# A gated recurrence and its feed-forward: stores in one transfer each, and one more block transposed by DMA

## The chip, the cores and the metric

The kernel runs on one core of a Trainium2 chip. The metric is the device time of one execution, in microseconds (us). Three runs of the kernel before took 178.43, 179.19 and 180.09 us; their median is 179.19.

## What is computed

A gated linear recurrence over 768 steps runs for 4 batches of 8 heads with 48 features each; its output, with the heads side by side as 384 columns, goes through a feed-forward layer with a SiLU:

```python
def _attn_ref(q, k, v, f_logit):                       # each (4, 8, 768, 48)
    f = 1.0 / (1.0 + np.exp(-f_logit))
    for t in range(S):
        state = f[:, :, t, :, None] * state + np.einsum('bhd,bhe->bhde', k[:, :, t], v[:, :, t])
        y[:, :, t] = np.einsum('bhd,bhde->bhe', q[:, :, t], state)

def _moe_ref(x, w_in, w_out):                          # x (3072, 384), w_in (384, 2048), w_out (2048, 384)
    h = x @ w_in
    g = h * (1.0 / (1.0 + np.exp(-h)))
    return g @ w_out
```

All inputs and the output are float32; the kernel's matmuls take bf16.

## The kernel before

The 768 steps are cut into 3 windows of 256, so that with 4 batches there are 12 blocks (block D is window D // 4 of batch D % 4). In a block each of 128 partitions holds two neighbouring steps (r = 0, 1), and the partitions fall into two chunks of 64 (f = 0, 1), each of 128 steps. Within a chunk the recurrence is done as masked matrix products; between chunks a state is carried on.

The order of all work is written out by hand, as a list of tokens (PLAN). A token is a kind, a block and, for most, the head half or chunk or column group; after an @ stands the engine (s SyncE's queue, v VectorE, a ScalarE, p GpSimd, called POOL). `emit` turns each into instructions, in the order of the list; each engine runs its own instructions in that order, and waits where data or buffers aren't ready. `uses` names the buffers that a token touches. Buffers come from pools of fixed size (SLOTS), freed at the last use; PSUM has eight banks.

The steps of a block, with the lines in the kernel before:

- ldf, ldk, ldq, ldv load a block's gate logits, k, q and v (L276). Block 0 and 1 are loaded in halves of four heads.
- E, L, F1 (L278 to L282), SA (L284), CS (L286 and L289, TensorE), IA, A, AX (L292 to L296), AM (L298) make the decay factors. E to AX are ScalarE's.
- K1 (L300) and Q1 (L302) scale k and q; KI (L306) and QG (L311) write them as bf16 to a tile named qk.
- TQ (L320) turns that tile on TensorE, eight transpositions of 128 x 128 into PSUM, and QC copies them to SBUF (L272). TD (L324) does the same as one DMA transpose on SyncE's queue. Blocks 0 to 3 go by TQ and QC, blocks 4 to 11 by TD.
- SC (L333) forms the scores of a head half, AT (L339) masks them, Y (L347) multiplies by v (cast by VB), YS (L354) adds the carried state's part, YC (L272) copies a chunk's output to the tile yb.
- YT (L362) turns yb on TensorE in three transpositions a chunk and XC copies them (L272); YD (L366) does it as one DMA transpose. Blocks 0 to 3 go by YT and XC, blocks 4 to 11 by YD.
- DP (L372), SD (L377) and SU (L379) carry the state to the next chunk.
- MI (L388) multiplies by a 256-column group of w_in: 8 tokens of 6 matmuls for a block. SI (L392) is the SiLU of that group, from PSUM to the bf16 tile hT. MO (L396) multiplies by w_out: 4 matmuls a token, four tokens for each of two output tiles of 128 rows. OC (L272) copies such a tile from PSUM, and SO (L402) stores both tiles of a block, or one.
- WI and WO load the weights in eight pieces each, and CI and CO cast them to bf16.
- W is a row of matmuls on an empty tile (L416) that fills waits of TensorE early in the run; its result is not used.

Rows of hT come out with the even steps of a chunk ahead of the odd ones, since that is how the transposed y lies. So an output tile holds them in that order, and SO needs two transfers, one for each r, of 64 partitions each (L401 and L402):

```python
dst = out.rearrange("(b w f p r) n -> b w r p f n", b=B, f=2, p=64, r=2)
for r in range(2):
    E.dma_start(out=dst[b, w, r][:, fs], in_=T[0][64 * r:64 * r + 64, fs])
```

All stores and loads are issued by SyncE. Whenever the order passes from an exponential or logarithm to a SiLU or back, ScalarE loads another function table (L420).

Of the kernel before, what the change touches and what calls it, by code (L numbers as in the profile page):

```python
# [36 lines left out]
    QG.2.1@v QG.2.0@v CI.7@v K1.2.1@v CI.4@p K1.2.0@v KI.2.1@v KI.2.0@v AM.2@v CI.0@v SA.3.0@v SA.3.1@p SU.1.1@p
    CO.0@p VB.2@p CO.5@p MI.0.1 MI.0.3 MI.0.5 MI.1.3 MI.0.2 MI.1.5 SI.0.1 SI.1.1 SI.1.3 SI.0.2 SI.1.5 MI.0.4 SI.0.4
    MI.0.7 MI.1.7 MI.1.4 SI.1.7 SI.0.5 TQ.2.1 TQ.2.0 CI.6@v QC.2.0@v QC.2.1@v CO.1@v MI.1.0 MI.0.0 SI.0.3 SI.1.4
    SI.1.2 SI.1.0 MI.0.6 SI.0.6 SI.0.0 MI.1.6 SC.2.1 SC.2.0 AT.2.1 AT.2.0 SI.1.6 CO.3@a CO.2@a SI.0.7 MO.1.0.0  # L40
    MO.0.1.0 MO.0.0.0 MO.1.1.0 MO.1.0.1 MO.0.0.1 MO.0.1.1 DP.2 Y.2.0 Y.2.1 SU.2.0@v CO.4@v MO.1.1.1 YS.2.1 CS.3.0
    SD.2.1 YC.2.0@v YC.2.1@v MO.1.0.2 MO.0.0.2 MO.0.1.2 YT.2.1 YT.2.0 XC.2.1@v XC.2.0@v IA.3.0 E.4.0 L.4.0 MO.1.1.2
    CS.3.1 SA.4.0@v MI.2.4 CS.4.0 CO.6@p CO.7@v MO.1.0.3 OC.1.0@v MO.0.1.3 MO.1.1.3 E.4.1 L.4.1 AX.3.1 F1.3.1 F1.3.0
    A.3.0 IA.4.0 A.4.0 SU.2.1@p SA.4.1@p CS.4.1 IA.3.1 A.3.1 IA.4.1 AX.4.0 AX.3.0 AX.4.1 F1.4.0 MO.0.0.3 K1.3.0@p
    K1.3.1@p KI.3.1@p Q1.3.0@v OC.0.1@v OC.1.1@v Q1.3.1@v QG.3.0@v AM.3@v QG.3.1@v AM.4@v ldq.4@s ldk.4@s MI.2.7
    MI.2.6 MI.2.3 A.4.1 F1.4.1 OC.0.0@a MI.2.1 MI.2.0 SI.2.7 SI.2.6 SI.2.0 SI.2.1 KI.3.0@v TQ.3.0 MI.2.5 TQ.3.1
    Q1.4.0@v Q1.4.1@v QG.4.1@v K1.4.1@p KI.4.1@p QG.4.0@v QC.3.1@v ldv.3@s ldf.6@s ldv.4@s ldf.5@s MI.2.2 MO.2.0.0
    SI.2.3 SI.2.4 SI.2.5 SI.2.2 QC.3.0@v K1.4.0@p KI.4.0@p VB.3@p VB.4@p SC.3.1 AT.3.1 SC.3.0 AT.3.0 MO.2.1.0
# [433 lines left out]
```

## Time and profile before

| What | us |
|---|---|
| median of three runs (lowest, highest) | 179.19 (178.43, 180.09) |
| the profiled execution, its own time | 178.64 |
| its span, from the first to the last instruction | 176.9 |
| TensorE matmuls busy | 168.7 (95% of the span) |
| ScalarE busy | 120.9 (68%) |
| VectorE busy | 103.0 (58%) |
| POOL busy | 62.1 (35%) |

The granted TensorE clock was 0.995 over the span. In the profile PE is TensorE's matmuls, PEld its weight loads (they overlap matmuls), DVE is VectorE, ACT ScalarE, POOL GpSimd and SP SyncE, whose queue issues the transfers (SPq). A group's row gives line, engine, operation, the tiles written and read, shapes and count, then busy us and mean ns of one, then the idle time of the engine ahead of them and what ended it. A row of the timeline gives start, length, engine, line and how many; consecutive instructions of a kind are merged. A row of stretches gives start and end, then each engine's busy time and count, the granted clock, the busy share of the 16 DMA engines, and GB/s.

### The profile page before, as it was taken

Reading aid. Unit: us, or ns where it says so; the run is one execution under the profiler, and the core shown is the slowest. Engines: PE = TensorE matmul, PEld = TensorE weight load, DVE = VectorE, ACT = ScalarE, POOL = GpSimd, SP = SyncE. Lnnn points to the kernel's source line nnn. Section 1 sums busy time; section 2 is a strip of 40 time slices with the busy share of each in tenths; the row PEclk is TensorE's granted clock in tenths of the full one; section 3 lists DMA queues with packets and bytes.
Section 4 is the critical chain, followed back from the end, with each engine's and each line's share of the span. In section 5 each row is a group of like instructions: output and inputs, shape, how many; then the busy total and the mean of one; then the engine's idle time right before and its main releaser. Section 6 shows DMA issues by size and latency. Waiting matters only on the chain.

```text
span 176.9 us, 5606 instructions
## 1 busy us (share of the span) xinstructions
PE 168.7 (95%) x2280; PEld 127.9 (72%) x2280; DVE 103.0 (58%) x252; ACT 120.9 (68%) x281; POOL 62.1 (35%) x106
## 2 busy tenths in 40 slices
PE   7598999999999999999999999999999999999990
PEld 5486789766796688857688767688676788875550
DVE  6269987636798996297484498880369710000320
ACT  5868999854799899888699985599902128772001
POOL 6387561133593683013728017507501000000000
PEclk9999999999999999999999999999999999999998
DMA  5999999999908959997999996999999461000094
GB/s 127 294 310 344 358 342 363 351 340 242 320 13 154 319 143 212 200 293 191 190 189 220 236 313 169 197 253 229 250 161 171 108 136 44 4 0 0 5 241 113
DMA packets 82234, 36.02 MB, mean 204 GB/s; under 512 B 74016, under 2 KB 82208, under 8 KB 82208
## 3 DMA queue, kind: packets, MB, share of 16 engines
q1 hardware_dynamic: 82208, 35.66, 81.4%
q8 instruction: 18, 0.29, 0.7%
q14 instruction: 8, 0.07, 0.1%
HBM read 25.17 MB, written 4.72 MB: 169 GB/s over the span
## 4 chain that ended last, share of the span: by engine, by line
PE 83%; issue 8%; DVE 3%; DMA 2%; ACT 2%; SPq 1%
PE ps L388 36%; PE ps L396 29%; PE ps L333 3%; PE ps L347 3%; PE ps L354 3%; PE ps L372 3%; DMA wide<-in_f_logit_dram 2%; PE ps L416 2%; PE ps L320 1%; PE ps L286 1%; DVE atm L339 1%; PE ps L362 1%; ACT e L278 1%; ACT lf L280 1%; SPq L276 1%
## 5 line engine op out<-in xcount | busy, mean ns | idle before, releaser
L396 PE MATMUL ps<-w_out_sb,hT 128*128 128x384 bf16 x384 | 67.5, 326 | 0.0
L388 PE MATMUL ps<-xT,w_in_sb 128*128 128x256 bf16 x576 | 65.5, 273 | 0.0
L388 PEld LDWEIGHTS <-w_in_sb 128*128 128x128 bf16 x576 | 55.6, 98 | 7.2
L392 ACT ACTIVATE hT<-ps 128x512 bf16<-128x512 f32 x96 | 49.9, 618 | 9.2 <-PE ps L388 8.7
L396 PEld LDWEIGHTS <-hT 128*128 128x128 bf16 x384 | 35.7, 98 | 22.0
L339 DVE TENSOR_TENSOR atm<-ps,mask 128x512 bf16<-128x512 f32 x48 | 30.0, 682 | 8.9 <-PE ps L333 7.6
L272 DVE COPY o<-ps 128x384 f32<-128x384 f32 x18 | 9.9, 554 | 29.1 <-issue 21.2
L306 POOL TENSOR_TENSOR qk<-wide,ia 128x192 bf16<-128x192 f32 x36 | 21.5, 621 | 11.0 <-ACT hT L392 7.2
L379 POOL TENSOR_TENSOR st<-sd,al 128x384 bf16<-128x384 f32 x12 | 10.2, 850 | 19.7 <-DVE sd L377 16.6
L311 DVE TENSOR_TENSOR qk<-wide,ps 128x192 bf16<-128x192 f32 x48 | 14.2, 347 | 3.7 <-ACT ps L294 3.2
L272 ACT CAST yb<-ps 128x384 bf16<-128x384 f32 x12 | 5.4, 480 | 14.5 <-PE ps L354 11.8
L278 ACT ACTIVATE e<-wide 128x384 f32<-128x384 f32 x24 | 12.3, 523 | 2.2 <-DMA wide<-in_f_logit_dram 2.0
L302 DVE SCALAR_TENSOR_TENSOR wide<-e,wide 128x192 f32<-128x192 f32 x24 | 11.2, 483 | 3.6 <-ACT f L282 3.6
L284 POOL TENSOR_TENSOR s<-lf 128x192 bf16<-128x192 bf16 x15 | 8.8, 593 | 11.8 <-ACT lf L280 10.4
L280 ACT ACTIVATE lf<-e 128x384 bf16<-128x384 f32 x24 | 12.0, 520 | 0.5
L377 DVE TENSOR_TENSOR sd<-ps,st 128x384 f32<-128x384 f32 x16 | 8.6, 552 | 6.1 <-PE ps L372 6.0
L272 ACT COPY o<-ps 128x384 f32<-128x384 f32 x6 | 2.9, 490 | 13.3 <-issue 12.4
L416 PE MATMUL ps<-idle 128*128 128x256 bf16 x72 | 10.8, 305 | 1.3 <-DVE idle L428 1.3
L420 ACT ACT_TABLE_LOAD x9 | 11.5, 1283 | 0.2
L300 POOL TENSOR_TENSOR wide<-wide,f 128x192 f32<-128x192 f32 x13 | 8.2, 631 | 8.4 <-ACT f L282 4.0
L292 ACT ACTIVATE ia<-ps 128x192 f32<-128x192 f32 x24 | 7.6, 333 | 4.2 <-PE ps L289 4.2
L416 PEld LDWEIGHTS <-idle 128*128 128x128 bf16 x72 | 7.3, 109 | 3.0 <-DVE idle L428 1.2
(59 smaller groups left out, 157.4 us busy)
## 6 DMA issues: line engine op xcount, KB each, us to landing
out_dram<-o SPq DMA_DIRECT2D x22, 192.0 KB, 3.1
wide<-in_f_logit_dram SPq DMA_DIRECT2D x10, 384.0 KB, 4.8
wide<-in_q_dram SPq DMA_DIRECT2D x10, 384.0 KB, 4.6
wide<-in_k_dram SPq DMA_DIRECT2D x10, 384.0 KB, 5.7
wide<-in_v_dram SPq DMA_DIRECT2D x10, 384.0 KB, 4.6
wide<-in_moe_w_in_dram SPq DMA_DIRECT2D x8, 384.0 KB, 6.3
wide<-in_moe_w_out_dram SPq DMA_DIRECT2D x8, 384.0 KB, 7.0
wide<-in_f_logit_dram SPq DMA_DIRECT2D x4, 192.0 KB, 3.3
```

The costliest lines, as they stand in the source:

```text
L272: copy = lambda o, i: E.copy(o, i) if eng == "a" else E.tensor_copy(o, i)
L278: nc.scalar.activation(T[1][:, hs], T[0][:, hs], AF.Exp, scale=-1.0)
L280: nc.scalar.activation(T[1][:, hs], T[0][:, hs], AF.Ln, bias=1.0)
L302: E.scalar_tensor_tensor(out=T[1][:, hs, 0:d], in0=T[0][:, hs, d:2 * d], scalar=1.0, in1=T[1][:, hs, 0:d], op0=ALU.add, op1=ALU.mult)
L306: E.tensor_mul(T[2][:, g, 1, :, r, :, 0:d], T[0][:, hs, r * d:r * d + d].rearrange("p (n x) d -> p n x d", x=2), T[1][:, hs].rearrange("p ...
L311: E.tensor_mul(T[2][:, g, 0, :, r, :, 0:d], T[0][:, hs, r * d:r * d + d].rearrange("p (n x) d -> p n x d", x=2), T[1][:, 0:4 * d].rearrang ...
L339: nc.vector.tensor_mul(T[2][:, g, x], T[x].rearrange("p (s n c) -> p s n c", s=2, n=2), mask.rearrange("p s r c -> p s (r c)")[:, :, None, ...
L388: nc.tensor.matmul(h[:, i, 128 * fs.start:128 * fs.stop], w_in_sb[:, j, kk, i * 128:i * 128 + 128], T[0][:, fs, kk], start=(kk == 0), stop ...
L392: nc.scalar.activation(T[1][:, 2 * j:2 * j + 2], T[0].rearrange("p (n c) -> p n c", n=2), AF.Silu)
L396: nc.tensor.matmul(T[1][:, 0:d_model], T[0][:, n, f * 128:f * 128 + 128], w_out_sb[:, n], start=(n == 0), stop=(n == NTILES - 1))
L416: nc.tensor.matmul(T[0][:, 0:256], idle[:, 0:128], idle[:, 0:256], start=True, stop=True, skip_group_check=True)
L420: nc.scalar.preload_act_table_set(turn[name])
```

## The change

Three parts of the program text change, and the order.

1. SI writes its 512 columns to hT with the steps in natural order: a column that stood at (f, r, c) goes to (f, c, r), so every second bf16 element of a row is written. An output tile then holds its rows in the order of the output, and SO is one transfer of 128 partitions.
2. The last output tile (block 11, second tile) is computed, copied and stored in two column parts, 0 to 255 and 256 to 383 (LAST).
3. Block 3 is turned by DMA: TQ.3, QC.3, YT.3 and XC.3 go, and TD.3.0, TD.3.1 and YD.3 come.
4. The list of tokens is another one. Every kind has the same number of tokens except those named here; many stand elsewhere or on another engine. Stores are issued by SyncE (13 SO tokens of two transfers before, 3 of one after), ScalarE (7 after) and POOL (4 after). The fillers go from 72 matmuls to 60. KI on VectorE goes from 6 to 10 of 24 (the rest is POOL's), YC on ScalarE from 12 to 6 of 24 (the rest is VectorE's), OC on ScalarE from 6 of 24 to 13 of 25, VB on POOL from 5 to 10 of 12.

```diff
+LAST = ((0, 256), (256, 384))
...
     if kind == "MO":
-        return [I("hT", D), I("ps", "o", D, a[1])]
+        return [I("hT", D), I("ps", "o", D, a[1], *a[3:])]
     if kind == "OC":
-        return [I("ps", "o", D, a[1]), I("o", D)]
+        return [I("ps", "o", D, *a[1:]), I("o", D, *a[2:])]
     if kind == "SO":
-        return [I("o", D)]
+        return [I("o", D, *a[2:])]
...
-    dst = out.rearrange("(b w f p r) n -> b w r p f n", b=B, f=2, p=64, r=2)
+    dst = out.rearrange("(b w f t) n -> b w t f n", b=B, f=2, t=128)
...
         elif kind == "SI":
             j = a[1]
-            nc.scalar.activation(T[1][:, 2 * j:2 * j + 2], T[0].rearrange("p (n c) -> p n c", n=2), AF.Silu)
+            nc.scalar.activation(T[1][:, 2 * j:2 * j + 2].rearrange("p n (f c r) -> p (n f) r c", f=2, r=2),
+                                 T[0].rearrange("p (m r c) -> p m r c", m=4, r=2), AF.Silu)
         elif kind == "MO":
-            f, m = a[1:]
+            f, m = a[1:3]
+            cols = slice(*LAST[a[3]]) if len(a) == 4 else slice(0, d_model)
             for n in range(4 * m, 4 * m + 4):
-                nc.tensor.matmul(T[1][:, 0:d_model], T[0][:, n, f * 128:f * 128 + 128], w_out_sb[:, n], start=(n == 0), stop=(n == NTILES - 1))
+                nc.tensor.matmul(T[1][:, 0:cols.stop - cols.start], T[0][:, n, f * 128:f * 128 + 128], w_out_sb[:, n, cols],
+                                 start=(n == 0), stop=(n == NTILES - 1))
         elif kind == "OC":
-            copy(T[1][:, a[1]], T[0][:, 0:d_model])
+            cols = slice(*LAST[a[2]]) if len(a) == 3 else slice(0, d_model)
+            copy(T[1][:, a[1], cols], T[0][:, 0:cols.stop - cols.start])
         elif kind == "SO":
             fs = slice(0, 2) if g is None else slice(g, g + 1)
-            for r in range(2):
-                E.dma_start(out=dst[b, w, r][:, fs], in_=T[0][64 * r:64 * r + 64, fs])
+            cols = slice(*LAST[a[2]]) if len(a) == 3 else slice(0, d_model)
+            E.dma_start(out=dst[b, w][:, fs, cols], in_=T[0][:, fs, cols])
```

The new order on VectorE from its first QG to YC.0.1, and SyncE's transfers from block 3's to block 6's:

```
VectorE: QG.1.1 Q1.0.1 QG.1.0 QG.0.1 K1.0.1 Q1.0.0 QG.0.0 AT.1.1 AT.1.0 AM.1 QC.0.0 SU.1.0 AT.0.0 AT.0.1 SU.0.0 AM.2
         YC.0.0 YC.0.1
SyncE:   k.3 q.3 k.4 q.4 v.3 TD.3.0 TD.3.1 v.4 f.5 TD.4.1 TD.4.0 f.6 YD.3 q.5 q.6 k.5 YD.4 k.6 v.6 TD.5.1 TD.5.0
         TD.6.1 TD.6.0
```

On TensorE from block 2's MI to the scores of block 4, and at the end:

```
MI.2.1 MI.2.7 MI.2.0 MI.2.3 MI.2.2 MI.2.4 MI.2.6 MO.2.0.0 MI.2.5 SC.3.0 MO.2.0.1 SC.3.1 MO.2.1.0 MO.2.0.2 DP.3
Y.3.0 Y.3.1 DP.4 YS.3.1 MO.2.0.3 SC.4.1
...
MO.10.0.3 MO.10.1.3 MO.11.1.0.0 MO.11.1.1.0 MO.11.1.2.0 MO.11.1.3.0 MO.11.1.0.1 MO.11.1.1.1 MO.11.1.2.1 MO.11.1.3.1
```

with OC.10.1, SO.10, OC.11.1.0 and SO.11.1.0 on ScalarE, and OC.11.1.1 on VectorE and SO.11.1.1 on SyncE last.

More of the change, by code (lines that the diff above doesn't have):

```diff
@@ L90 @@
[L90 to L92 removed]
+    ldf.1.0@s E.1.0 L.1.0 SA.1.0@v W.19:CS.1.0 CS.1.0 W.8:CS.1.1 ldf.0.1@s E.0.1 L.0.1 ldf.1.1@s ldf.0.0@s ldq.1.1@s
+    IA.1.0 E.1.1 A.1.0 L.1.1 SA.1.1@v E.0.0 ldq.1.0@s ldk.1.1@s F1.1.0 L.0.0 F1.1.1 Q1.1.0@v Q1.1.1@v SA.0.0@v CS.1.1
+    W.3:CS.0.0 CS.0.0 IA.1.1 F1.0.1 F1.0.0 IA.0.0 ldq.0.1@s ldk.1.0@s ldk.0.1@s ldk.0.0@s ldq.0.0@s SA.0.1@p CS.0.1
@@ L93 @@
+    SI.10.3 MO.9.0.0 MO.9.0.1 MO.9.0.2 MO.9.1.0 MO.9.0.3 SI.11.0 MO.11.0.0 MI.10.0 MO.9.1.1 MO.9.1.2 SI.10.0 SI.10.2
+    SI.11.6 MO.11.0.1 MO.11.0.2 MO.11.0.3 MO.9.1.3 MO.10.1.0 MO.10.0.0 MO.10.0.1 MO.10.1.1 MO.10.1.2 MO.10.0.2
+    OC.11.0@v OC.9.0@v SO.11.0@s OC.9.1@a SI.10.6 MO.10.0.3 MO.10.1.3 SO.9@a MO.11.1.0.0 MO.11.1.1.0 MO.11.1.2.0
+    MO.11.1.3.0 OC.10.0@v OC.10.1@a SO.10@a OC.11.1.0@a SO.11.1.0@a MO.11.1.0.1 MO.11.1.1.1 MO.11.1.2.1 MO.11.1.3.1
+    OC.11.1.1@v SO.11.1.1@s
 """
```

128 lines of the change are left out of this document (60 added, 68 removed).

## The prediction

> **What bounds the kernel now.** I read the page first, then TensorE's timeline, the chain of work that ended last, and VectorE's groups in the stretch before TensorE fills up.
>
> ```profile
> span 176.9 us, 5606 instructions
> ...
> PE 168.7 (95%) x2280; PEld 127.9 (72%) x2280; DVE 103.0 (58%) x252; ACT 120.9 (68%) x281; POOL 62.1 (35%) x106
> ...
> PE 83%; issue 8%; DVE 3%; DMA 2%; ACT 2%; SPq 1%
> ...
> L396 PE MATMUL ps<-w_out_sb,hT 128*128 128x384 bf16 x384 | 67.5, 326 | 0.0
> L388 PE MATMUL ps<-xT,w_in_sb 128*128 128x256 bf16 x576 | 65.5, 273 | 0.0
> ```
>
> The chain is TensorE's for 83% of the span; the 8% called issue is one piece of 12.43 us at the end which the timeline fills with matmuls. The two great groups never sat idle before a matmul (0.0).
>
> ```profile
> 1.25 4.85 PE L416 MATMUL ps<-idle 128*128 128x256 bf16 x28 [1.25 <-DVE idle L428]
> 7.88 0.24 PE L286 MATMUL ps<-s,tri 128*128 128x192 bf16 x1 [1.78 <-POOL s L284]
> 22.89 7.41 PE L388 MATMUL ps<-xT,w_in_sb 128*128 128x256 bf16 x66
> 64.05 9.33 PE L388 MATMUL ps<-xT,w_in_sb 128*128 128x256 bf16 x84
> 73.76 0.64 PE L333 MATMUL ps<-qkT 48*64 48x128 bf16 x32
> 158.81 13.81 PE L396 MATMUL ps<-w_out_sb,hT 128*128 128x384 bf16 x84
> ```
>
> So the time has three parts: a front up to 22.89 us, in which TensorE waits for its first blocks and runs fillers; a solid stretch from 22.89 to 172.62 us (158.81 + 13.81), 149.7 us of matmuls without a hole; and a tail of 4.3 us to the end of the span. Matmuls overlap in the timeline, so prices are taken from the chain, whose pieces add up:
>
> ```profile
> 51.06 0.45 PE ps L320 x8
> 143.92 11.79 PE ps L388 x108
> 172.70 0.48 ACT o L272
> ```
>
> One transposition of 128 columns costs 0.45/8 = 0.056 us, one matmul of 256 columns 11.79/108 = 0.109, one of 384 columns about (13.81-0.33)/84 = 0.160 (0.33 being the last one's drain).
>
> **The solid stretch.** Block 3 loses TQ.3.0, TQ.3.1 (8 transpositions each) and YT.3.0, YT.3.1 (3 each): 22 x 0.056 = 1.23 us of TensorE. All of it stands on the path, since nothing there is idle. Their evictions go too (two QC, two XC, on VectorE and ScalarE, both with time to spare: 58% and 68% busy) and are counted at nothing. The last output tile is cut into 256 and 128 columns: 16 x (0.109 + 0.056) = 2.64 in place of 16 x 0.160 = 2.57, so +0.07. Eight PSUM evictions, state updates, casts and the like change engines both ways (VectorE 10 KI for 6, ScalarE 6 YC for 12, POOL 10 VB for 5); they are covered as long as none is late for a matmul. One is by my walk: CO.0 now stands on ScalarE behind twelve SiLUs and ends some 0.2 us after the first MO could start. Sum of the stretch: -1.23 + 0.07 + 0.2 = -0.96.
>
> **The front.** Between VectorE's first QG and its YC.0.1, after which XC.0 and the unbroken MI stream follow, VectorE is the engine that is hardly ever free:
>
> ```profile
> 9.73:22.66 12.93, 12.04 (x28) 1.00 1.13 339
> ```
>
> ```profile
> L311 DVE TENSOR_TENSOR qk<-wide,ps 128x192 bf16<-128x192 f32 x8 | 2.4, 349 | 1.5 <-ACT ps L294 1.4
> L306 DVE TENSOR_TENSOR qk<-wide,ia 128x192 bf16<-128x192 f32 x2 | 1.1, 564 | 0.0
> L284 DVE TENSOR_TENSOR s<-lf 128x192 bf16<-128x192 bf16 x2 | 0.5, 246 | 0.0
> L272 DVE COPY xT<-ps 128x384 bf16<-128x384 bf16 x1 | 0.3, 347 | 0.0
> L298 DVE TENSOR_TENSOR al<-ar,own 128x16 f32<-128x16 f32 x1 | 0.2, 161 | 0.0
> ```
>
> ```profile
> L302 DVE SCALAR_TENSOR_TENSOR wide<-e,wide 128x192 f32<-128x192 f32 x24 | 11.2, 483 | 3.6 <-ACT f L282 3.6
> ...
> L300 DVE TENSOR_TENSOR wide<-wide,f 128x192 f32<-128x192 f32 x11 | 3.7, 351 | 0.7 <-DMA wide<-in_k_dram 0.7
> ```
>
> ```profile
> 1.85 3.75 DMA wide<-in_f_logit_dram
> ```
>
> The first row is that stretch: 12.04 us busy of 12.93. Of the groups in it, KI.0.1 (1.1), two SA (0.5) and XC.1.1 (0.3) leave the list in the new order; Q1.0.1, K1.0.1 and one AM (0.48 + 0.35 + 0.16; the two rows after the groups are the whole run's) enter it: 12.04 - 1.9 + 1.0 = 11.1. It begins when A.1.1 is done. Walking ScalarE's new list (E.1.1 after the third f load, which lands at 1.85 + 3.75 = 5.60 today, then 14 short activations) I get 9.8 for that, against 9.73. So YC.0.1 ends at 20.9 with no wait inside, at 21.8 with the 0.9 us of waiting that stands there today; 22.66 today. POOL's side of the same walk (KI.1.1, KI.1.0, KI.0.1, KI.0.0, VB.1 one behind the other) is done in time. I take -0.9, as today's waits seem nearer than none, with -1.7 and, should POOL come one KI late (half of 1.1), -0.4 as ends. Fillers drop from 72 to 60; they fill waits and count nothing.
>
> **The tail.** Today the last copy (384 columns, 0.48 us on ScalarE, row above) ends at 173.18, and two stores follow, one behind the other, on SP:
>
> ```profile
> 171.78 2.53 SPq L402 DMA_DIRECT2D out_dram<-o  x3
> ```
>
> ```profile
> L402 SPq DMA_DIRECT2D out_dram<-o x26: 466/603/2252, 73.6 to 173.7; - x26
> ...
> DMA to landing us min/median/max: 2.1/3.1/5.2
> ```
>
> ```profile
> L272 DVE COPY o<-ps 128x384 f32<-128x384 f32 x18 | 9.9, 554 | 29.1 <-issue 21.2
> ```
>
> The second issue ends at 174.31, some 1.1 us after the copy; its landing and the closing come after. With one transfer the second issue, 0.6 us by the median, goes. The copy shrinks to 128 columns on VectorE: 0.28 by a line through its 554 ns at 384 and 349 at 192 columns; so -0.2 and, with a smaller transfer at the 2.1 end of the landing range, -0.85 in all. The 256-column part is copied and stored from ScalarE during the last 16 x 0.056 = 0.9 us of matmuls, so it lands first. At most -1.1 (landing shorter still), at least -0.2 (only the copy).
>
> **Sum:** -0.96 - 0.9 - 0.85 = -2.7 us. The profiled execution took 178.64 (span 176.9 and 1.7 around it), so 175.9 on its own scale; the median of the three runs, 179.19, is 0.55 higher, and on that scale I forecast 176.5. A measurement here tells about 1% (1.8 us) from no change, so this is a gain not far beyond the bound.
>
> **What is added elsewhere.** Two TD and one YD for block 3 go through SP's queue and the DMA engines, where both are short of time (the second fence is the landing of the 16 TD):
>
> ```profile
> 63.86 1.25 SPq L366 DMA_TRANSPOSE xT<-yb  x1
> ...
> 66.35 5.70 SPq L324 DMA_TRANSPOSE qkT<-qk  x4
> ```
>
> ```profile
> DMA to landing us min/median/max: 3.2/3.9/5.8
> ```
>
> ```profile
> 45.00:50.00 5.00, 5.00 (x42) 3.75 (x40) 4.26 (x14) 3.98 (x14) 3.79 (x7) 1.00 0.89 245
> 50.00:64.00 14.00, 14.00 (x277) 10.35 (x276) 12.90 (x28) 13.05 (x33) 9.20 (x15) 1.00 0.74 180
> 64.00:80.00 16.00, 16.00 (x214) 12.61 (x214) 11.21 (x27) 13.84 (x30) 4.85 (x8) 1.00 0.94 215
> 100.00:120.00 20.00, 20.00 (x286) 14.61 (x287) 17.46 (x44) 15.30 (x43) 7.48 (x13) 1.00 0.97 237
> ```
>
> A TD holds the queue 5.70/4 = 1.43 us, a YD 1.25: 4.1 us more. Idle DMA time between 45 and 64 us is 5 x 0.11 + 14 x 0.26 = 4.2 us: it just fits. TD.3.0 can issue at about 44.5 us, lands by 50.5 even at 5.8, and SC.3.0 stands at 51.7 in my walk: hidden. Behind TD.3 on SP wait v.4, f.5 and TD.4; TD.4.1 then lands near 54 and SC.4.1 stands at 56.6. Next late is block 5: the new VectorE list gives KI.6.0 last, TD.5.0 lands near 71.7 and SC.5.0 stands at 72.3; today the pair SC.5 at 73.76 comes some 2.4 us after its tile. That is the thinnest cover.
>
> The 26 stores on SP become 14: 3 on SP, 7 on ScalarE's queue, 4 on POOL's. On ScalarE each holds the engine for about an SP issue, 0.6 us. The covering slack is in the SiLU stages, here one of them:
>
> ```profile
> 26.24 3.04 ACT L392 ACTIVATE hT<-ps 128x512 bf16<-128x512 f32 x6
> ```
>
> ```profile
> L392 ACT ACTIVATE hT<-ps 128x512 bf16<-128x512 f32 x96 | 49.9, 618 | 9.2 <-PE ps L388 8.7
> ...
> L278 ACT ACTIVATE e<-wide 128x384 f32<-128x384 f32 x24 | 12.3, 523 | 2.2 <-DMA wide<-in_f_logit_dram 2.0
> ...
> L292 ACT ACTIVATE ia<-ps 128x192 f32<-128x192 f32 x24 | 7.6, 333 | 4.2 <-PE ps L289 4.2
> ...
> L272 ACT COPY qkT<-ps 128x1024 bf16<-128x1024 bf16 x3 | 3.0, 1010 | 2.4 <-PE ps L320 2.4
> ```
>
> SiLUs follow each other every 3.04/6 = 0.51 us, MI groups every 6 x 0.109 = 0.655: 0.15 us to spare for each, so a store is made good after four. On POOL no store is seen in this trace: between 0.6 (SP's median issue) and 2.25 us (SP's longest), near the first since SP's issues mostly are; SO.1 stands there ahead of SA.11.1, which CS.11.1 needs.
>
> To let rows of the output leave in one transfer, the SiLU now writes every second bf16 of a tile row. No row shows such a write. Bounds: 618 ns (as many elements, so no gain), and the 1010 ns of the copy that covers as many addresses, 1024. I take 618, as the element count sets the durations here (192 columns 333 ns, 384 columns 523). Of this the Trainium skill, page SBUF — State Buffer, section Door 1: The DMA port swizzle (why `[64,N]` ≈ `[32,N]`), says that accesses keep full bandwidth while at least two fall into one 16-byte line, so up to a stride of 8 bf16; by it the term is nothing and the sum stays -2.7, and by the upper row it would be the last rival below; no run yet shows it.
>
> **Rivals.**
> - A transposed tile is late (place: SC.5.0 or SC.6.0). A landing at 5.8 in place of 3.9 is 1.9 late, the cover 0.6: TensorE stands 1.3. Time 176.5 + 1.3 = 177.8. For it: the cover; against it: in the trace before no SC waited on a TD.
> - The transfers become the bound (slower). Place: 45 to 140 us, where the DMA share is 0.74 to 1.02 of the time. If the 4.1 us don't find the idle time, loads and later tiles slip by them, TensorE's earlier start is no use either, and only the tail is kept: 179.19 + 4.1 - 0.85 = 182.4. It decides from about 2.7 us of slip that later stretches don't win back. Against it: my walk of SP's list finds tiles ahead of SC.7 to SC.11.
> - POOL's stores hold it. At 2.25 us each instead of 0.6, SA.11.1 and, after SO.5, the state update SU.11.0 come 1.65 later, on covers of about 1: 0.65 each, 177.8. VectorE is busy 17.46 of 20 us in the stretch of SO.1 (row above). Beside it the Trainium skill, page SBUF — State Buffer, section A bandwidth-pool intuition that's wrong (but worth ruling out), tells of a DMA issued from GpSimd that grew from 620 to 3100 ns beside a VectorE copy, as GpSimd can't write descriptors while VectorE holds a shared port. By that figure the two places would cost an estimated 2 x (3.1 - 0.6 - 1) = 3 us, so 179.5; no run yet shows it.
> - The spread SiLU is slow. At 1010 ns, follow-on 0.9 us, each of 96 SiLUs passes the 0.655 of its MI by 0.245; of 23 us perhaps 18 stay after the MO stages: 194. It decides from a follow-on of 0.655.
>
> **How the numbers follow.** Forecast 0.50, own range 174.8 to 177.5 (ends of front and tail, and 0.3% of spread); late tile 0.17; transfers 0.15; POOL 0.10; SiLU 0.08. The range 174.8 to 181.2 takes in the first, second and fourth and the near part of the third, and leaves out 0.19. Faster by over 1% (below 177.4): 0.50. Slower by over 1% (above 181.0): SiLU and nearly all of the transfers, 0.22. Between: 0.28.
>
> **What would show it.** Right: MI's unbroken stream begins near 22 us; no idle before L333 groups; the SiLU group's mean stays near 618; TensorE ends near 171, and 3.5 us of tail. Wrong: SC waiting for DMA qkT; holes in TensorE between 45 and 110 us; a SiLU mean over 740; a stretch from 22 us to the last matmul longer than 149.7.

## The result and the profile after

The changed kernel took 181.7 us (median of 4, 181.42 to 182.7) beside 179.06 for the kernel before, measured with it: a ratio of 1.0146 (95% interval 1.011 to 1.0183). It is slower; the forecast was 176.5, a ratio of 0.985. The profiled execution took 181.42 us on its own, with a span of 179.7 and a granted clock of 1.0.

First the page of the kernel after, the lines that answer to those of the page before:

```profile
span 179.7 us, 5549 instructions
...
PE 168.6 (94%) x2262; PEld 127.2 (71%) x2262; DVE 103.2 (57%) x253; ACT 129.2 (72%) x279; POOL 63.7 (35%) x108
...
PE 54%; ACT 20%; DMA 11%; SPq 5%; DVE 3%; issue 3%; POOL 2%; ACTq 0%; DVEq 0%; POOLq 0%
...
L394 ACT ACTIVATE hT<-ps 128x512 bf16<-128x512 f32 x96 | 60.0, 800 | 10.8 <-PE ps L390 10.5
L390 PE MATMUL ps<-xT,w_in_sb 128*128 128x256 bf16 x576 | 66.0, 273 | 0.6 <-DMA xT<-yb 0.4
```

TensorE has the same work as before (168.6 us busy), but the chain is TensorE's for 54% of the span and no longer 83%; ScalarE is now on it. The SiLU group has grown from 618 to 800 ns apiece, 10.1 us in all. MI, which never sat idle, now does.

The three parts of the time, from TensorE's timeline and from the stretches (start and end, then each engine's busy time):

```profile
22.27 7.49 PE L390 MATMUL ps<-xT,w_in_sb 128*128 128x256 bf16 x66
...
167.83 8.82 PE L400 MATMUL ps<-w_out_sb,hT 128*128 128x384 bf16 x69
```

```profile
22.27:176.65 154.38, 151.21 (x1961) 113.32 (x1958) 87.06 (x201) 112.15 (x235) 49.98 (x77) 1.00 0.84 199
```

The stretch of the kernel before, for comparison:

```profile
22.89:172.62 149.73, 149.73 (x1967) 112.90 (x1964) 86.54 (x199) 103.44 (x238) 48.00 (x75) 1.00 0.81 193
```

The front ends at 22.27 us (22.89 before: -0.62). The last matmul ends at 176.65 and the span at 179.7, so the tail is 3.05 us (4.3 before: -1.25). Both are gains, as forecast. The stretch between them was to shrink from 149.73 to 148.8 us and has grown to 154.38. That is the whole failure: 5.6 us, with 3.2 us in which TensorE ran nothing (154.38 - 151.21), where before there was none. The other 2.4 us are counted as busy time (151.21 in place of 148.8). A matmul is counted to its modelled end, 273 ns for MI, while in an unbroken row the next one starts after 109 ns; so a hole costs more than the idle time shown for it.

What TensorE waited for after 22 us, by the waits (total us, times, longest):

```profile
PE ps L335 <- ACT hT L394: 1.0, 3, 0.4
PE ps L335 <- DMA qkT<-qk: 0.4, 1, 0.4
PE ps L390 <- DMA xT<-yb: 0.4, 1, 0.4
PE ps L374 <- ACT hT L394: 0.3, 1, 0.3
...
```

The scores (L335) and the state products (L374) read no hT. They wait for SiLUs because they need a PSUM bank that a SiLU still reads. Of the eight rows, four (1.7 us) are for a SiLU and two (0.8 us) for a transfer; the four left out are of 0.2 us each. Two theories follow: the spread SiLU is the cause, or the new order is, with transposed tiles and stores in the wrong places. In the expectations the second is split by place. Of the runs below only e7_before_td3 has slower executions (three of six, more than 1.5% above its fastest): its time and ratio are those of the other three, and its trace is of a slower one.

### The profile page after: what moved, and what is told of

Its sections match the earlier page's. It is cut to its first block, busy times and chain, and to the rows that moved or that the text cites. A ratio compares the mean times of both kernels' runs of the same rounds, so it can differ in the third digit from the quotient of the medians.

```text
span 179.7 us, 5549 instructions
## 1 busy us (share of the span) xinstructions
PE 168.6 (94%) x2262; PEld 127.2 (71%) x2262; DVE 103.2 (57%) x253; ACT 129.2 (72%) x279; POOL 63.7 (35%) x108
## 4 chain that ended last, share of the span: by engine, by line
PE 54%; ACT 20%; DMA 11%; SPq 5%; DVE 3%; issue 3%; POOL 2%; ACTq 0%; DVEq 0%; POOLq 0%
PE ps L400 28%; PE ps L390 17%; ACT hT L394 14%; DMA wide<-in_q_dram 8%; SPq L278 4%; DMA xT<-yb 3%; PE ps L349 2%; PE ps L356 2%; PE ps L335 2%; SPq L326 1%; PE ps L374 1%; POOL qk L308 1%; DVE wide L304 1%; ACT lf L282 1%; ACT L426 1%
## 5 line engine op out<-in xcount | busy, mean ns | idle before, releaser
L400 PE MATMUL ps<-w_out_sb,hT 128*128 128x384 bf16 (+2 forms) x400 | 68.2, 320 | 0.5 <-ACT w_out_sb L274 0.2
L394 ACT ACTIVATE hT<-ps 128x512 bf16<-128x512 f32 x96 | 60.0, 800 | 10.8 <-PE ps L390 10.5
L274 DVE COPY o<-ps 128x384 f32<-128x384 f32 (+1 forms) x12 | 6.3, 528 | 29.2 <-issue 26.1
L308 POOL TENSOR_TENSOR qk<-wide,ia 128x192 bf16<-128x192 f32 x28 | 17.1, 634 | 4.2 <-DVE wide L302 3.5
L274 ACT CAST yb<-ps 128x384 bf16<-128x384 f32 x6 | 2.9, 476 | 14.1 <-PE ps L356 13.5
L381 POOL TENSOR_TENSOR st<-sd,al 128x384 bf16<-128x384 f32 x9 | 7.5, 835 | 14.3 <-PE ps L390 5.6
L274 ACT COPY o<-ps 128x384 f32<-128x384 f32 (+1 forms) x13 | 6.0, 477 | 8.8 <-PE ps L400 8.8
L274 POOL CAST vb<-wide 128x768 bf16<-128x768 f32 x10 | 8.2, 826 | 8.9 <-DMA wide<-in_v_dram 5.8
L335 PE MATMUL ps<-qkT 48*64 48x128 bf16 x384 | 9.6, 221 | 1.7 <-ACT hT L394 1.0
L274 DVE CAST yb<-ps 128x384 bf16<-128x384 f32 x18 | 9.5, 549 | 2.6 <-PE ps L356 2.6
```

Source lines behind the costliest of these rows:

```text
L274: copy = lambda o, i: E.copy(o, i) if eng == "a" else E.tensor_copy(o, i)
L308: E.tensor_mul(T[2][:, g, 1, :, r, :, 0:d], T[0][:, hs, r * d:r * d + d].rearrange("p (n x) d -> p n x d", x=2), T[1][:, hs].rearrange("p ...
L335: nc.tensor.matmul(sc[x][64 * f:64 * f + 64, s, n], T[0][lo:lo + d, g, 1, n, s, 64 * f:64 * f + 64], T[0][lo:lo + d, g, 0, n, :, 64 * f:64 ...
L394: nc.scalar.activation(T[1][:, 2 * j:2 * j + 2].rearrange("p n (f c r) -> p (n f) r c", f=2, r=2), T[0].rearrange("p (m r c) -> p m r c", ...
L400: nc.tensor.matmul(T[1][:, 0:cols.stop - cols.start], T[0][:, n, f * 128:f * 128 + 128], w_out_sb[:, n, cols], start=(n == 0), stop=(n == ...
```

## The experiments

All ratios are to the kernel before, measured beside each run. They are not quotients of the medians, and differ from these by up to 0.5%. The median of the kernel before lay between 179.06 and 179.54 us, so for rows that were not measured together the ratios are the surer comparison. With single transfers and a contiguous SiLU the rows of the output come out in another order (even steps ahead of odd ones), with the same bytes; those runs serve for timing alone.

| Run | Order | SiLU | us (lowest, highest) | ratio [95%] |
|---|---|---|---|---|
| changed kernel | new | spread write | 181.7 (181.42, 182.7) | 1.0146 [1.011, 1.0183] |
| e1_plain_silu | new | contiguous | 179.44 (178.57, 180.38) | 1.0006 [0.9978, 1.0034] |
| e13_silu_read_only | new | spread read | 179.12 (178.39, 180.65) | 0.9979 [0.9954, 1.0005] |
| e5_store_sync | new, SO.0 moved | contiguous | 178.48 (177.41, 179.36) | 0.996 [0.9933, 0.9988] |
| e6_store_and_sc6 | and SC.6.0 | contiguous | 178.0 (177.09, 179.42) | 0.9951 [0.992, 0.9981] |
| e10_v5_early | and ldv.5 | contiguous | 177.25 (177.01, 177.45) | 0.9896 [0.9871, 0.9921] |
| e14_all_mended | as e10 | spread read | 177.02 (176.6, 177.55) | 0.9858 [0.9828, 0.9887] |
| e15_mended_spread | as e10 | spread write | 180.56 (180.33, 181.37) | 1.0063 [1.0039, 1.0088] |
| e8_order_tq3 | new, block 3 on TensorE | contiguous | 183.2 (182.56, 184.61) | 1.025 [1.0215, 1.0285] |
| e2_before_spread | before, one-transfer stores | spread write | 179.78 (179.29, 180.14) | 1.0033 [1.0016, 1.005] |
| e3_before_one_store | before, one-transfer stores | contiguous | 178.54 (177.66, 178.99) | 0.9964 [0.9944, 0.9983] |
| e11_silu_read | before, one-transfer stores | spread read | 178.3 (177.73, 179.69) | 0.9952 [0.9926, 0.9977] |
| e16_before_tail | as e11, last tile split | spread read | 177.61 (177.26, 177.82) | 0.9887 [0.986, 0.9914] |
| e9_before_td3_qk | as e3, TD.3 | contiguous | 178.72 (177.79, 180.43) | 0.998 [0.9952, 1.0008] |
| e7_before_td3 | as e3, TD.3 and YD.3 | contiguous | 183.52 (183.11, 185.51) | 1.0287 [1.0233, 1.0341] |

Two more, on where else the rows could be put in order, stand at the end. The profiled executions of e5, e6 and e13 lie in the upper part of their runs, so their holes are rather large for their medians.

### Which of the two, SiLU or order

e1_plain_silu, the changed kernel with the SiLU of before:

```diff
-            nc.scalar.activation(T[1][:, 2 * j:2 * j + 2].rearrange("p n (f c r) -> p (n f) r c", f=2, r=2),
-                                 T[0].rearrange("p (m r c) -> p m r c", m=4, r=2), AF.Silu)
+            nc.scalar.activation(T[1][:, 2 * j:2 * j + 2], T[0].rearrange("p (n c) -> p n c", n=2), AF.Silu)
```

> The changed kernel with the SiLU writing its columns side by side again; stores stay single transfers, so the rows of the output come out in another order (even steps ahead of odd ones), with the same bytes. Theory 1 (the spread SiLU, 0.58 us from start to start against 0.48 before, holds PSUM banks and so TensorE): most of the 5.6 us lost in the solid stretch comes back, time 176.5 to 178, TensorE's last matmul near 171.5 to 172.5. Theory 2 (the new order's transfers, with block 3 by DMA and stores on other queues, make tiles late): 180.5 to 181.7, with the waits for DMA xT and DMA qkT still there and the ones behind the SiLU gone at little gain.

e2_before_spread is the opposite: the order of before, with the new SiLU and one-transfer stores, all on SyncE. e3_before_one_store is e2 with the old SiLU.

```diff
-            for r in range(2):
-                E.dma_start(out=dst[b, w, r][:, fs], in_=T[0][64 * r:64 * r + 64, fs])
+            E.dma_start(out=dst[b, w][:, fs], in_=T[0][:, fs])
```

> The kernel before, in its own order, with the spread SiLU and single-transfer stores (on SyncE's queue) alone. Theory 1: the SiLU's mean goes from 618 to about 800 ns there too and the time to 181 to 184, in spite of 0.6 us less tail. Theory 2: the SiLU's price is hidden, 178 to 179.

> The kernel before with single-transfer stores alone, SiLU side by side, so rows of the output in another order. Both theories: the tail is 0.4 to 0.8 us shorter, the rest unchanged: 178.3 to 178.8. If stores of 128 partitions cost the transfers more than pairs of 64, above 179.

Neither theory held alone. The SiLU gives back 2.3 us in the new order (181.7 to 179.44) and costs 1.2 us in the old (178.54 to 179.78). Some 3 us against the forecast stay with the order. The SiLU groups of e2 and e3:

```profile
L392 ACT ACTIVATE hT<-ps 128x512 bf16<-128x512 f32 x96 | 59.7, 802 | 5.2 <-PE ps L388 5.1
```

```profile
L392 ACT ACTIVATE hT<-ps 128x512 bf16<-128x512 f32 x96 | 50.1, 617 | 9.5 <-PE ps L388 9.1
```

The jump in the write costs 0.18 us a SiLU, whatever the order. How little of these 9.6 us comes out depends on what stands behind a stage of SiLUs.

### The order's places: a store, a tile, a load

In e1_plain_silu, ScalarE's timeline and TensorE's behind it read:

```profile
84.88 2.99 ACTq L407 DMA_DIRECT2D out_dram<-o  x1
...
87.98 0.36 ACT L284 ACTIVATE f<-lf 128x192 f32<-128x192 bf16 x1 [2.31 <-issue]
...
94.28 3.24 ACT L394 ACTIVATE hT<-ps 128x512 bf16<-128x512 f32 x6
```

```profile
92.71 1.71 PE L390 MATMUL ps<-xT,w_in_sb 128*128 128x256 bf16 x12 [0.17 <-ACT o L274]
94.93 3.33 PE L390 MATMUL ps<-xT,w_in_sb 128*128 128x256 bf16 x29 [0.51 <-ACT hT L394]
```

The store SO.0 is issued from ScalarE's queue for 2.99 us, ScalarE stands 2.31 of them, and the SiLUs of block 6 begin late, so MI.6 runs out of PSUM banks. e5_store_sync moves that one store:

```diff
-SO.0@a
+SO.0@s
```

> The new order with the contiguous SiLU of e1_plain_silu (output rows stand in the permuted order), and one more edit: the store of block 0 is issued by SyncE instead of ScalarE, at the same place of the order. Theory 'a store on ScalarE holds back the SiLUs behind it': in e1_plain_silu TensorE stood 1.25 us around MI.6.4, MI.6.3 and MI.6.2, while ScalarE was late with its first SiLUs; those three holes go, and the time falls from 179.4 to 178.2 to 178.5. Rival 'ScalarE would be late there in any case, by its other work': the holes stay and the time is 179.2 to 179.6. A third way: SyncE's queue holds ldk.7 and the transposition YD.5 back behind the store, and MI.5 waits for it: 179.4 or above.

About 0.9 us less, as the first theory had it, though the intervals of the two ratios overlap a little. The rows are the clearer sign: in place of the two broken MI rows stands one, whole:

```profile
89.73 8.46 PE L390 MATMUL ps<-xT,w_in_sb 128*128 128x256 bf16 x76
```

What TensorE waited for in e5 now begins with a tile and two casts of v:

```profile
PE ps L335 <- DMA qkT<-qk: 1.2, 1, 1.2
PE ps L374 <- POOL vb L274: 0.7, 1, 0.7
PE ps L374 <- ACT vb L274: 0.5, 1, 0.5
```

e6_store_and_sc6 gives the tile cover; e10_v5_early moves the load.

```diff
-TD.6.1 TD.6.0 SC.6.1 SC.6.0 ldv.5@s ... AT.6.1 AT.6.0 VB.5@a AM.6@p SU.6.0@p MO.3.0.0 MO.3.0.1 MO.3.0.2
+TD.6.1 TD.6.0 SC.6.1 ldv.5@s ... VB.5@a AM.6@p SU.6.0@p AT.6.1 MO.3.0.0 MO.3.0.1 SC.6.0 AT.6.0 MO.3.0.2
```

> As e5_store_sync, and SC.6.0 (which waited 1.01 us for the last transposition of block 6 in e1_plain_silu) stands behind MO.3.0.0 and MO.3.0.1, with the mask products AT.6.1 and AT.6.0 moved to suit. Output rows stand in the permuted order. Theory 'each transposed tile needs cover in front of its first reader, and the new order gives too little at block 6': 0.8 to 1.0 us below e5_store_sync. Rival 'the work behind it (VB.5, Y.6) is late anyhow, by the same queue of transfers': within 0.3 us of e5_store_sync, with the hole moved to DP.5 or Y.6.

```profile
PE ps L374 <- ACT vb L274: 1.2, 1, 1.2
PE ps L288 <- DVE yb L274: 0.8, 1, 0.8
```

The median fell by 0.5 us only (0.2 by the ratios, whose intervals overlap), and the first row of e6 shows why: DP.5, next in line, waits for VB.5, as its rival said. The second, a wait for an eviction on VectorE, was not followed up. SyncE's timeline of e6 has the cause of the first:

```profile
69.61 5.39 SPq L326 DMA_TRANSPOSE qkT<-qk  x4
75.05 0.58 SPq L278 DMA_DIRECT2D wide<-in_v_dram  x1
```

Four transpositions hold the queue for 5.4 us, and the load of v of block 5 stands behind them.

```diff
-ldk.6@s ldv.6@s ... TD.6.1 TD.6.0 SC.6.1 ldv.5@s
+ldk.6@s ldv.6@s ldv.5@s ... TD.6.1 TD.6.0 SC.6.1
```

> As e6_store_and_sc6 (178.0; output rows permuted), and the load of v of block 5 is issued ahead of the four transpositions of blocks 5 and 6 instead of behind them. Theory 'the hole of 1.34 us at DP.5 in e6_store_and_sc6 is the transpositions standing ahead of ldv.5 in SyncE's queue': the hole goes, and the time falls by 0.8 to 1.3, to 176.7 to 177.2. Rival 'the load, put ahead, delays the transpositions of block 5 by its own 1.2 us, and SC.5 waits instead': 177.8 to 178.4.

0.75 us less at the median, just short of the theory's 0.8 (1.0 by the ratios). The runs spread over 2.3 us in e6 (twelve runs) and 0.4 here (four). A single wait of 0.3 us is left there, and one of 0.4 at Y.2.0:

```profile
PE ps L349 <- DVE atm L341: 0.4, 1, 0.4
PE ps L374 <- ACT vb L274: 0.3, 1, 0.3
```

### Block 3 by DMA, alone

e7_before_td3 puts TD.3 and YD.3 into the order of before, where TQ.3 stood and behind YC.3:

```diff
-TQ.3.0 MI.2.5 TQ.3.1 ... QC.3.1@v ... QC.3.0@v ... YT.3.1 YT.3.0 XC.3.1@a XC.3.0@a
+TD.3.1 TD.3.0 MI.2.5 ... YC.3.1@a YC.3.0@a YD.3 ldf.7@s
```

> The order of the kernel before with single-transfer stores on SyncE and the contiguous SiLU (as e3_before_one_store, 178.54; output rows permuted), and block 3 alone turned by DMA: TD.3 and YD.3 in place of TQ.3, QC.3, YT.3 and XC.3. Theory 'turning a block by DMA saves its 22 transpositions at 0.056 us where the transfers have cover': minus 1.2, plus up to 0.3 at MI.3.5 for YD.3: 177.3 to 177.7. Rival 'the two or three transfers of 1.3 us each on SyncE put later loads and transpositions off by as much as is saved': 178.3 to 179.

By the ratios 3.2% more than e3, some 5.8 us (5.0 by the medians), far worse than either theory. (The 7.7 us in the next expectation are from the median of all six executions.) Its waits in an execution of 187.79 us, and SyncE's timeline:

```profile
PE ps L388 <- DMA xT<-yb: 4.2, 1, 4.2
PE ps L372 <- POOL vb L272: 2.9, 1, 2.9
```

```profile
50.09 2.70 SPq L324 DMA_TRANSPOSE qkT<-qk  x2
52.89 0.53 SPq L276 DMA_DIRECT2D wide<-in_v_dram  x1
```

In e3 the same load of v went out earlier:

```profile
42.17 1.10 SPq L276 DMA_DIRECT2D wide<-in_v_dram  x1
```

TD.3 waited in the queue for its data, and four loads behind it went out some 10 us later than in e3; VB was late by that, and YD.3, issued behind four other loads, landed late for MI.3. So e9_before_td3_qk puts TD.3 behind the loads and leaves y on TensorE:

```diff
-TQ.3.0 MI.2.5 TQ.3.1 ... QC.3.1@v ldv.3@s ldf.6@s ldv.4@s ldf.5@s ... QC.3.0@v
+MI.2.5 ... ldv.3@s ldf.6@s ldv.4@s ldf.5@s TD.3.1 TD.3.0 ...
```

> The order of the kernel before with single-transfer stores and the contiguous SiLU (e3_before_one_store, 178.54; output rows permuted), and q and k of block 3 alone turned by DMA, issued behind ldv.3, ldf.6, ldv.4 and ldf.5, so that no load waits behind them; y of block 3 is turned on TensorE as before. Theory 'what cost e7_before_td3 its 7.7 us was the queue (loads and the y behind transpositions that wait for their data), not the transposition itself': 16 transpositions at 0.056 us less, 0.9, and up to 0.4 given back at SC.3.1: 177.6 to 178.1. Rival 'every 1.3 us transfer on SyncE in this stretch puts off the loads of blocks 5 and 6 and comes back as a hole at TensorE': 178.6 to 181.

The loss is gone. Since e9 moves TD.3 and also leaves YD.3 out, it doesn't tell the two apart; it shows that turning q and k by DMA costs nothing of that size once no load stands behind it, and that it is the queue is argued from the rows above. A gain isn't seen either: 0.998 beside 0.9964 for e3, the intervals overlapping, and a median (178.72) in the rival's range. One wait has come that e3 did not have, and it takes back most of the estimated 0.9 us (16 x 0.056) that the transpositions saved:

```profile
PE ps L333 <- DMA qkT<-qk: 0.6, 1, 0.6
```

e8_order_tq3 undoes block 3 in the new order:

```diff
-TD.3.0 TD.3.1 ... SI.2.2 MI.2.6 MO.2.0.0 ... YD.3 ... MO.2.1.2 MO.2.1.3
+SI.2.2 TQ.3.1 MI.2.6 TQ.3.0 QC.3.1@v QC.3.0@v MO.2.0.0 ... MO.2.1.2 YT.3.1 XC.3.1@a YT.3.0 XC.3.0@v MO.2.1.3
```

> The new order with the contiguous SiLU of e1_plain_silu (179.44; output rows permuted), and block 3 turned on TensorE again: TQ.3 and QC.3 among the MI.2, YT.3 and XC.3 ahead of MO.2.1.3. Theory 'block 3 by DMA is a gain in this order too': 1.2 us more TensorE work, less 0.5 for the two holes at MI.3.1 and MI.3.3 if these come from it: 180.0 to 180.7. Rival 'block 3 by DMA is what delays the later transfers': the holes at MI.3 and SC.6.0 go (1.6 us) and the time is 178.8 to 179.4.

It came out 3.8 us above e1, beyond both ranges, and says little of block 3: the added XC.3.0 stands ahead of AT.4 on VectorE, and Y.4 waits for that.

```profile
PE ps L349 <- DVE atm L341: 1.9, 2, 1.5
```

### Whether the parts add, and a SiLU that costs nothing

The rows can also be put in order where the SiLU reads:

```diff
-            nc.scalar.activation(T[1][:, 2 * j:2 * j + 2].rearrange("p n (f c r) -> p (n f) r c", f=2, r=2),
-                                 T[0].rearrange("p (m r c) -> p m r c", m=4, r=2), AF.Silu)
+            nc.scalar.activation(T[1][:, 2 * j:2 * j + 2].rearrange("p n (f c r) -> p (n f) c r", f=2, r=2),
+                                 T[0].rearrange("p (m r c) -> p m c r", m=4, r=2), AF.Silu)
```

e11_silu_read has it in the order of before, e13_silu_read_only in the changed kernel with no other edit.

> The order of the kernel before with single-transfer stores; the SiLU puts the rows in order by reading PSUM with a jump (f32, every 64th element) and writes its output without one. If the spread SiLU of the change is slow because of the jump in its write, this is as fast as e3_before_one_store: 178.4 to 178.9, mean SiLU 618 ns. If any jump costs, on either side: as e2_before_spread, 179.5 to 180.

> The changed kernel with one edit: the SiLU reads PSUM with the jump and writes without it, so that rows come out in order as in the changed kernel. If the jump in the SiLU's write is the cause of the part of the loss that e1_plain_silu gave back: as e1_plain_silu, 179.2 to 179.8, mean SiLU 600 to 620 ns. If e1's gain had come from the permuted rows at the store or elsewhere: 181 to 182.

Both came out as if the SiLU were contiguous. The group of e13, with rows in the order of the output:

```profile
L394 ACT ACTIVATE hT<-ps 128x512 bf16<-128x512 f32 x96 | 50.3, 610 | 15.3 <-PE ps L390 14.1 <-ACT hT L394 0.6
```

e14_all_mended is e13 with the three edits of the order, e15_mended_spread the changed kernel with the three edits alone.

> The changed kernel with the SiLU of e13_silu_read_only and the three edits of the order of e10_v5_early (the store of block 0 on SyncE, SC.6.0 behind MO.3.0.1, the load of v of block 5 ahead of the transpositions). If the loss lies in these four places: as e10_v5_early, 177.0 to 177.6, within 1 us of the forecast of 176.5 and below the kernel before. If the jump in the read of PSUM hurts in this tighter order: 178 to 179.

> The changed kernel as it is, spread SiLU and all, with the three edits of the order alone. If SiLU and order add: 181.7 less the 2.2 that the three edits brought with the plain SiLU (179.4 to 177.25), 179.3 to 179.7. If the slow SiLU sets the pace by itself once the other holes are gone: 180.5 to 181.5.

e14 is the fastest kernel of all by median and ratio, at 177.02 us and with all parts of the change in it (its interval overlaps those of e10 and e16). e15 lies at the lower end of its second range, so the two parts do not add: the slow SiLU costs 3.5 us in the mended order (180.56 against 177.02), 2.6 in the changed one (181.7 against 179.12; by the ratios 3.0), 1.5 in the old one (e2 against e11). In these three pairs it costs more the tighter the rest is. Of the two longest waits of e15, with the three places mended, the first is for SiLUs:

```profile
PE ps L335 <- ACT hT L394: 1.0, 3, 0.4
PE ps L374 <- ACT vb L274: 0.5, 1, 0.5
```

e16_before_tail has the split of the last tile alone, on top of e11 (its edit is the new order's last MO.11.1, OC.11.1 and SO.11.1 tokens).

> The order of the kernel before with single-transfer stores, the SiLU that reads PSUM with the jump (e11_silu_read, 178.3), and the split of the last output tile alone. If the split gives the 1.25 us that the tail of the changed kernel lost: 177.0 to 177.5. If most of that came from the ScalarE stores of the last tiles, which stay on SyncE here: 177.8 to 178.3.

It gave 0.7 us against e11 by the medians, between its two ranges, and 1.2 us by the ratios (0.9887 and 0.9952). The first theory counted on too much: e11 has the single transfers already, and from the last matmul to the end of the span it takes 3.5 us, not 4.3; with the split it is 2.9. The rival is tested in part only, as ScalarE issues the store of the first part here too (SO.11.1.0@a).

### Rows put in order by TensorE

e4_mi_read is the changed kernel with MI reading its moving columns in natural order, neighbours 128 bytes apart; e12_matmul_write is e3 with MI writing its columns two f32 apart.

```diff
-                                     T[0][:, fs, kk],
+                                     T[0][:, fs, kk].rearrange("p f (r c) -> p f c r", r=2),
```

```diff
-                    nc.tensor.matmul(h[:, i, 128 * fs.start:128 * fs.stop],
+                    nc.tensor.matmul(h[:, i, 128 * fs.start:128 * fs.stop].rearrange("p (f c r) -> p f r c", c=64, r=2),
```

> The changed kernel with the steps put in natural order elsewhere: the matmul with w_in reads its moving columns in the order (f, c, r), every second read 128 bytes on, and the SiLU writes side by side. Output in the right order. Theory 1: as the first kernel, 176.5 to 178, if TensorE reads such columns at full rate (0.109 us for 256 columns). If it reads them slower, the w_in group's 65 us grow and the time with them. Theory 2: 180.5 or more.

> The order of the kernel before with single-transfer stores and the contiguous SiLU; the first multiplication of the feed-forward part puts the rows in order, by writing its columns to PSUM with a jump of two f32. If TensorE's write to PSUM takes the jump at full rate: as e3_before_one_store, 178.4 to 178.9, mean matmul 278 ns. If it halves the rate as the strided read of e4_mi_read did: 215 to 255.

253.72 us (ratio 1.417, 1.4135 to 1.4205) and 239.19 us (1.3369, 1.3326 to 1.3411). The MI groups, of e4 and then of e12:

```profile
L390 PE MATMUL ps<-xT,w_in_sb 128*128 128x256 bf16 x576 | 142.7, 405 | 0.0
```

```profile
L388 PE MATMUL ps<-xT,w_in_sb 128*128 128x256 bf16 x576 | 126.9, 420 | 0.0
```

142.7 and 126.9 us in place of 65.5: TensorE pays for a jump on either side, about double.

## Why the prediction was wrong, by its steps

**The front, -0.9.** Right: -0.62, inside its ends, and in the way that was walked: VectorE ended YC.0.1 at 21.94 us (22.66 before). The unbroken MI stream began at 22.1 to 22.4 us in the traces of the new order (e14: 22.23; e4 apart, whose matmuls are slow), and at 22.9 to 24.1 in those of the order of before (before 22.89, e16 23.40, e11 24.11). So the trace of before is an early one, and nothing finer than a microsecond can be read.

**The tail, -0.85.** Right in mechanism, too small: -1.25, past the -1.1 given as the most. The runs split it: with the single transfer alone it is 3.5 us (e3 and e11), so the second issue, put at -0.6, was worth -0.8; with the last tile cut as well it is 2.9 (e16) to 3.05, so copy and landing, put at -0.25, were worth some -0.5. The rows of the kernel after:

```profile
175.79 0.37 ACT L274 COPY o<-ps 128x256 f32<-128x256 f32 x1 [1.27 <-PE ps L400]
176.19 0.35 ACTq L408 DMA_DIRECT2D out_dram<-o  x1
176.75 0.29 DVE L274 COPY o<-ps 128x128 f32<-128x128 f32 x1 [2.75 <-PE ps L400]
```

The copy was put at 0.28 and took 0.29; the last store landed 1.5 us after its issue, below the 2.1 us that bounded it.

**The stretch, -0.96: the step that failed,** at +4.65. Four sentences of the working go with it.

- "I take 618, as the element count sets the durations here." The SiLU with the jump takes 800 ns; the count of elements didn't change, the form of the write did. The bounds (618, 1010) held the value, but the forecast was made at one end and the rival at the other, and the middle was never priced.
- "It decides from a follow-on of 0.655." It decided earlier. ScalarE's timeline, of the kernel after and of e14:

```profile
25.30 7.30 ACT L394 ACTIVATE hT<-ps 128x512 bf16<-128x512 f32 x12
32.29 0.98 ACT L274 CAST w_out_sb<-wide 128x768 bf16<-128x768 f32 x1
```

```profile
25.27 6.23 ACT L394 ACTIVATE hT<-ps 128x512 bf16<-128x512 f32 x12
31.32 0.89 ACT L274 CAST w_out_sb<-wide 128x768 bf16<-128x768 f32 x1
```

  The SiLUs follow each other every 0.59 us ((7.30 - 0.80) / 11), which is below the 0.655 of an MI group. But they begin 3.0 us after MI (25.30 against 22.27) and must catch up. At 0.51 they win 0.14 a group, at 0.59 only 0.06; so the twelve end 1.1 us later, CO.0 behind them too, and the PSUM banks that the next scores need. What counts is the last SiLU of a stage, not the pace. By the ratios this is 1.7 of the 2.9 per cent between the changed kernel and e14 (after to e13), and the remaining 1.2 is the order (e13 to e14). Taken the other way round, by e15, it is 0.8 for the order and 2.1 for the SiLU: the two don't add.
- "On ScalarE each holds the engine for about an SP issue, 0.6 us," and "a store is made good after four." Most of the seven did take less; SO.0 took 1.93 us in the kernel after and 2.99 in e1. The row of before that gave 603 ns as the median also gave 2252 as the longest; the prediction used that end for POOL's stores and not for ScalarE's.
- "It just fits," and "TD.5.0 lands near 71.7." Idle DMA time was there (its share in the stretch rose only from 0.81 to 0.84), so the rival that the transfers become the bound fell. The sum set the 4.1 us of SyncE's queue against the idle time of the engines, which are two different things; what was short was order in one queue. In the kernel after, SyncE between 60 and 76 us waits, and then issues:

```profile
SPq L326 <- DVE qk L308: 2.5, 1, 2.5
```

```profile
69.84 5.39 SPq L326 DMA_TRANSPOSE qkT<-qk  x4
75.29 0.58 SPq L278 DMA_DIRECT2D wide<-in_v_dram  x1
```

  The second of the four, TD.5.0, went out at 71.2 and landed at 74.5, 2.8 us later than the walk had it. The walk priced KI on VectorE but not the load of v, which stands behind all four. The late tile at SC.6.0 was a rival, with the right place, 1.3 us as its price, and 0.17 for its chance; it was 0.4 us in the kernel after and 1.2 in e5. That it would come together with a late load, a held ScalarE and a slow SiLU was left out: the rivals were priced as if only one could happen.

Even mended, the stretch doesn't show the -0.96: in e14 it is 149.92 us, from the row below, against 149.73 before.

```profile
22.23:172.15 149.92, 149.57 (x1961) 112.71 (x1958) 88.03 (x201) 102.55 (x235) 49.50 (x76) 1.00 0.85 203
```

So e14 gains by its front and tail (-0.66 and -1.25), and not in the stretch. That its ratio, 0.9858, comes out beside the forecast's 0.985 is luck in part, since the stretch gave nothing. Where it loses its gain can be summed from TensorE's records, each matmul taken from its start to the start of the next. The transpositions did shrink as forecast, from 2.47 us before to 1.26 in e14. Against that stand 0.4 us at DP.5, which waits for VB.5; 0.3 us inside MI, where some starts are held up; and about 0.5 us for two more changes between the wide matmuls (128 x 128, as MI and MO) and the narrow ones (SC, DP, Y, YS), 20 in each direction in place of 18. A change from MO to SC takes 0.256 us to the next start, where MO to MO takes 0.162; a change back takes 0.149, where SC to SC takes 0.014 on average. The prediction had no term for such changes. e9, which found no gain from 16 of the 22 transpositions, agrees.

**POOL's stores, a rival.** Not borne out. Their issues (shortest, median, longest ns), and their landing:

```profile
L408 POOL DMA_DIRECT2D out_dram<-o x4: 725/748/887, 110.5 to 138.3; - x4
...
DMA to landing us min/median/max: 3.2/4.4/5.2
```

After 22 us no instruction of TensorE waited for POOL. The page SBUF — State Buffer of the Trainium skill, section A bandwidth-pool intuition that's wrong (but worth ruling out), tells of a DMA issued from GpSimd that grew from 620 to 3100 ns beside a VectorE copy. The issues here stayed within 887 ns, with VectorE busy 57% of the span; no run here tells whether one of them stood beside such a copy.

**The rule on strides.** The same page of the Trainium skill, section Door 1: The DMA port swizzle (why `[64,N]` ≈ `[32,N]`), lets bf16 be strided by up to 8 for free. ScalarE's write with a stride of 2 went from 618 to 800 ns, so for this write the measurement decides against it. The same section of the Trainium skill also says that non-contiguous patterns in PSUM slow matmuls, and that agrees: e12's MI took 126.9 us in place of 65.5.

## What to carry to other kernels

A stage that trails another engine is priced by when its last instruction ends, from its start and its follow-on together; a follow-on below the leader's pace is no cover if the stage starts late and PSUM banks are waiting at its end. Before a transfer is added to a queue, walk what stands behind it: the transpositions themselves cost little here, and the loads and transfers behind them cost about 3% in e7. A matmul moved between two of another shape has a price of its own (about 0.23 us there and back here). When elements must change places, try the jump on each side of each instruction that touches them: of four places three cost 0.18 us an instruction or doubled TensorE's time, and one was free.

## What was new about the hardware

- ScalarE's 128x512 SiLU from PSUM to bf16 took 598 to 618 ns with both sides contiguous, 799 to 802 with every second bf16 written, and 610 to 618 with f32 read 256 bytes apart.
- TensorE's 256-column matmul took, by busy time over count, 0.114 us with contiguous columns (65.5 / 576), 0.248 with moving columns read 128 bytes apart (142.7 / 576), and 0.220 with f32 columns written 8 bytes apart (126.9 / 576).
- A store issued from ScalarE's queue took 0.35 to 0.38 us from 135 us on, in the kernel after and in e1, and 1.93 and 2.99 near 85 us, where loads were under way; in e1 ScalarE did nothing else for 2.31 of the 2.99.
- In e14 a change between TensorE's wide and narrow matmuls cost about 0.23 us there and back: 0.256 in place of 0.162 to the next start on the way there, 0.149 in place of 0.014 on the way back.
- In the profiled execution of e7, one of its longer ones, the granted clock fell while TensorE stood 4.2 us; no other execution that left a trace has such a hole or such a clock. The stretches of e7, with the clock third from the end:

```profile
64.00:72.00 8.00, 3.82 (x76) 2.62 (x68) 4.56 (x12) 2.96 (x11) 4.05 (x7) 0.82 1.14 226
72.00:78.00 6.00, 6.00 (x41) 4.66 (x40) 3.39 (x13) 3.33 (x9) 2.71 (x5) 0.67 0.75 147
```

  The 0.67 is a mean: in stretches of 2 us the clock is 0.78 from 68 to 70, about 0.50 from 70 to 76 and 1.00 from 76 on. A hole of 2.9 us before it, up to 60.2, left the clock at 1.00. Whether the hole is the cause was not tested apart, and only this execution shows it.
